# Gate logits of an attention + mixture-of-experts kernel, with gate weights and values swapped on TensorE

## The chip, the cores and the metric

One core of a Trainium2 chip runs the whole program. The metric is the device time of one execution in microseconds; smaller is better. TensorE is called PE below, its weight loads PEld, VectorE DVE, ScalarE ACT, GpSimd POOL, and SyncE, which here only issues transfers, SP.

## What is computed

The reference, cut to what matters:

```python
scores = scale * q @ k.T                     # 8 batches, 8 heads, 576 positions, head_dim 64
attn   = softmax(where(0 <= row - col < 64, scores, -1e9))
x      = (attn @ v) -> [4608, 512]           # heads side by side
logits = x @ w_gate                          # 8 experts
noisy  = logits + log1p(exp(x @ w_noise)) * noise
top2, top2_w = two largest of noisy, softmax over the two
out[row] += top2_w * (relu(x[row] @ w1[e]) @ w2[e])      # for the row's two experts
```

Everything is fp32. `x @ w_gate` and `x @ w_noise` together are 16 numbers for each row. Since `x` is a weighted sum of rows of `v`, the kernel multiplies `v` by the gate weights first (16 numbers for each key and head) and lets the attention weights sum those, as 16 extra columns beside the 64 value columns and one column of ones: attention's last product has 85 columns for a group of heads.

## The kernel before

The program has two stages. In the **attention stage** a loop over `j` (L761 on) handles 36 tiles: 9 blocks of 64 positions by 4 pairs of batches. One step of the loop holds parts of several tiles, so that each engine finds work: scores of tile `j`, softmax of `j` and `j-1`, transposes of `j-1`, the product with the values of `j-2`, normalising and the gate of `j-3`, storing `j-4`. Each engine executes its own instructions in the order in which the program issues them. In the **expert stage**, from about 182 us on, the eight experts' products run on PE, three chunks of rows for each expert, with rows gathered by POOL's indirect transfers.

In one step, PE's order is: `scores(j)` (L264, 16 matmuls on 64 x 64 quarters of the array), `pv(j-2)` (L323, 32 matmuls on such quarters), `transp(j-1)` (L300, four 128 x 128 transposes), `logits(j)` (L234). The trace shows two rows for each fp32 matmul, each with its weight load, and one for a transpose.

`logits(j)` is four matmuls. Stationary is one 128 x 128 slice of the turned values `VT` (128 contraction rows: two heads' dims, and 128 columns: the 64 keys of each of the pair's two sequence halves), moving are 64 gate-weight columns `wgx_sb`. The result is [128 keys, 256] in the shared PSUM tile `ps_g`, of which each half of the partitions needs half of the columns. `logits_copy(j)` (L240) takes the needed halves with two ACT copies of 64 partitions x 128 elements into slot 4 of the value tile `VW`, which `pv(j)` reads two steps later.

The softmax of a tile crosses the engines in this order: ACT copies the scores (`soft_a`, L274), DVE puts in the other block's columns (`soft_max`, L282) and takes the maximum (L287), POOL subtracts it (L288), ACT takes the exponential (`soft_b`, L292, in the step after), PE transposes (L300), DVE multiplies by the two masks (`apply_mask`, L305), PE takes the product with the values (L323, in the step after that). ACT's order in one step is `soft_b(j-1)`, `soft_a(j)`, eight scalings `norm_b(j-3)` (L342), the two copies L240, and, in steps 8 to 15, splitting an expert's weights (L215). Work of routing (L422 to L479) and POOL's scatters of row numbers (L482) are put between these in fixed portions.

SP issues the loads of queries (L93), keys (L97), values (L106), turned values (L112, for tile `j+2` into one of two buffers, after `logits(j)` has read it) and the stores of rows (L345).

Of the kernel before, what the change touches and what calls it, by code (L numbers as in the profile page):

```python
# [8 lines left out]
F32 = mybir.dt.float32  # L9
# [4 lines left out]
AF = mybir.ActivationFunctionType  # L14
# [49 lines left out]
def tile_kernel(ctx, tc, qT, kT, vx, vT, wgx, noise, w1, w2, out):  # L64
    nc = tc.nc
# [16 lines left out]
    wk = at.enter_context(tc.tile_pool(name="wk", bufs=2))  # L82
# [4 lines left out]
    VW = [acon.tile([128, 2, 5, 2, 4, 17], F32, name=f"vw{j}") for j in range(NP)]  # L87
    QC, VT = {}, {}

    def load_q(j):  # L90
        i, bp = divmod(j, NP)
        QC[j] = ld.tile([128, H, 64], F32, name="qc", bufs=3)
        nc.sync.dma_start(QC[j], qT[bp, :, i])  # L93

    def load_k(j):
        i, bp = divmod(j, NP)
        nc.sync.dma_start(KW[:, bp, i % 2], kT[bp, :, i])  # L97
# [6 lines left out]
    def load_v(j):  # L104
        i, bp = divmod(j, NP)
        nc.sync.dma_start(VW[bp][:, i % 2, 0:4], vx[bp, i])  # L106


    def load_vt(j):
        i, bp = divmod(j, NP)  # L110
        VT[j] = ld.tile([128, 4, 128], F32, name="vt", bufs=2)
        nc.sync.dma_start(VT[j], vT[bp, i])  # L112
# [3 lines left out]
    wgx_sb = acon.tile([128, 2, 64], F32)  # L116
# [11 lines left out]
    idle = ps.tile([128, 512], F32, name="ps_g")  # L128

    def warm(n):  # L130
        for _ in range(n):
            nc.tensor.matmul(idle[:, 384:512], lhsT=ones, rhs=ones, start=True, stop=True)

    warm(10)
    ident = consts.tile([128, 128], F32)
# [70 lines left out]
    def load_w1(e, ks=slice(0, KD), fs=slice(0, F)):  # L206
        if e < E:
            nc.sync.dma_start(w1s[:, ks, fs], w1[e][:, ks, fs])

    def load_w2(e, ks=slice(0, KF)):  # L210
        if e < E:
            nc.sync.dma_start(w2s[:, ks], w2[e][:, ks])
# [10 lines left out]
        return [lambda f=f: split(w2s[:, f], W2["h"][:, f], W2["l"][:, f]) for f in range(KF)]  # L223


    VG = idle[:, 0:256].rearrange("p (n c) -> p n c", n=1)

    def logits(j):
        p = VG[:, 0]
        x = VT.pop(j)  # L230
        for u in range(2):
            for g in range(2):
                q = u * 2 + g
                nc.tensor.matmul(p[:, q * 64:q * 64 + 64], lhsT=x[:, q, :], rhs=wgx_sb[:, g], start=True, stop=True)  # L234

    def logits_copy(j):
        i, bp = divmod(j, NP)
        for a in range(2):
            h = slice(a * 64, a * 64 + 64)
            nc.scalar.activation(VW[bp][h, i % 2, 4, :, :, 0:16].rearrange("p u (g x) e -> p (u g) x e", x=2),  # L240
                                 VG[h, 0].rearrange("p (k a x e) -> p k a x e", a=2, x=2, e=16)[:, :, a], AF.Copy)

    ST, T, P, TP, PT, XT = {}, {}, {}, {}, {}, {}

# [340 lines left out]
    def turn(e, c):  # L585
        pool = (exa, EXB.get("p"))[work.index((e, c)) % 2]
        xh = pool.tile([128, KD, WIDE], F32R, name="xh")
        xl = pool.tile([128, KD, WIDE], F32R, name="xl")
        XH[e, c], XL[e, c] = xh, xl
        cur = {}  # L590

        def f(q, m):
            if e:
                y = exa.tile([128, m // 32, KD, 32], F32, name="xy", bufs=2)
                nc.vector.transpose(y.rearrange("p t k c -> p (t k c)"),
                                    XG[e, c, q][:, :m // 32].rearrange("p t d -> p (t d)"))
                cur[q] = y.rearrange("p t k c -> p k t c")
            else:
                y = turn_bank()[:, :KD * m].rearrange("p (k m) -> p k m", k=KD)
                for k in range(KD):  # L600
                    nc.tensor.transpose(y[:, k], XG[e, c, q][:m, k * 128:k * 128 + 128], ident[:m, :m])
                cur[q] = y.rearrange("p k (t c) -> p k t c", c=32)

        def g(q, m):
            h, l = (x[:, :, q * 128:q * 128 + m].rearrange("p k (t c) -> p k t c", c=32) for x in (xh, xl))
            nc.scalar.activation(h, cur[q], AF.Copy)  # L606
            nc.vector.tensor_tensor(l, cur[q], h.bitcast(F32), op=OP.subtract)  # L607
        return [lambda q=q, m=m, x=x: x(q, m) for q, m in tiles(c) for x in (f, g)]
# [90 lines left out]
    def drain(n):  # L699
        calls[0] += 1  # L700
        while n and pending and calls[0] > calls[1]:
            f = next(pending[0], None)
            if f == HOLD:
                calls[1] = calls[0] + f
            elif f:
                f()
                n -= 1
            else:
                pending.pop(0)
# [5 lines left out]
    def drain_slots(n):  # L715
        for f in slots[:n]:
            f()
        del slots[:n]
# [4 lines left out]
    def ahead(n):  # L723
        for _ in range(n):
            if j >= NT and len(taken) < AHEAD:
                next(up00)
                taken.append(1)


    def rate(q):  # L730
        n = next(b for a, b in RATE if j < a)
        return (q + 1) * n // SLOTS - q * n // SLOTS
# [5 lines left out]
    def on(f, j, *a):  # L738
        if 0 <= j < NT:
            f(j, *a)  # L740

    for j in range(NT + 3):
        if j == TURN:
            for q, f in enumerate(turn(0, 0)):
                aux.setdefault(j + q // 2, []).append(f)

        if 0 < j < NT - 3:
            load_k(j + 3)
        on(store, j - 4)
        if j < 2:  # L750
            load_v(j + 2)
        if NT - 2 <= j < NT + 2:
            load_w2(0, slice((j - NT + 2) * 2, (j - NT + 3) * 2))
        on(norm_a, j - 3)
        drain(rate(0))
        on(scores, j)
        if j < NT - 3:
            load_q(j + 3)
        if W1G // 2 - 4 <= j < W1G // 2 + 4:
            k = j - W1G // 2 + 4  # L760
            load_w1(0, slice(k // 2, k // 2 + 1), slice(k % 2 * F // 2, (k % 2 + 1) * F // 2))  # L761
        if 2 < j < 3 + len(REST):
            REST[j - 3]()
        on(soft_b, j - 1)
        on(soft_a, j)
        ahead(2)
        drain(rate(1))
        on(pv, j - 2)
        on(norm_b, j - 3, 0)
        on(soft_max, j)  # L770
        on(soft_max2, j)
        drain_slots(1)
        if j < NP:
            warm(WARM)
        on(transp, j - 1)
        ahead(2)
        on(logits, j)
        if j < NT - 2:
            load_vt(j + 2)
        on(norm_b, j - 3, 1)  # L780
        on(apply_mask, j - 1)
        drain(rate(2))
        on(logits_copy, j)
        ahead(2)
        on(gate, j - 3)
        drain(rate(3))
        drain_slots(1 + j % 2)
        for f in aux.get(j, ()):
            f()
        drain(rate(4))  # L790
# [174 lines left out]
```

## Time and profile before

| | |
|---|---|
| Time, median of 3 runs | 1070.56 us (1070.03 to 1078.17) |
| Span of the profiled execution, first to last instruction | 1073.4 us |
| Attention stage, first to last `logits` of the 36 steps | 7.8 to 180.9 us |
| PE busy / PEld busy | 94% / 84% of the span |
| DVE / ACT / POOL busy | 41% / 38% / 50% of the span |
| Moved by DMA | 133.42 MB, 124 GB/s over the span |

How to read it: a row of a timeline gives the start in us, the duration, engine, line, operation, tile written <- tiles read, how many instructions were merged, and in brackets the idle time ahead of it with what ended that. A row of a group gives busy time, mean ns of one, and the idle time before. Windows give the busy time of each engine in a stretch, the granted PE clock (1.00 is full speed), and the mean busy share of the 16 DMA engines. Ends of matmuls are modelled, so starts are compared with starts.

### The profile page before, as it was taken

Reading aid. Unit: us, or ns where it says so; the run is one execution under the profiler, and the core shown is the slowest. Engines: PE = TensorE matmul, PEld = TensorE weight load, DVE = VectorE, ACT = ScalarE, POOL = GpSimd, SP = SyncE. Lnnn points to the kernel's source line nnn. Section 1 sums busy time; section 2 is a strip of 40 time slices with the busy share of each in tenths; the row PEclk is TensorE's granted clock in tenths of the full one; section 3 lists DMA queues with packets and bytes.
Section 4 is the critical chain, followed back from the end, with each engine's and each line's share of the span. In section 5 each row is a group of like instructions: output and inputs, shape, how many; then the busy total and the mean of one; then the engine's idle time right before and its main releaser. Section 6 shows DMA issues by size and latency. Waiting matters only on the chain. (4 is left out here: it accounts for less than half of the span.)

```text
span 1073.4 us, 19954 instructions
## 1 busy us (share of the span) xinstructions
PE 1012.5 (94%) x8025; PEld 906.9 (84%) x8025; DVE 444.7 (41%) x943; ACT 403.1 (38%) x1011; POOL 534.6 (50%) x612
## 2 busy tenths in 40 slices
PE   9877888899969999999999999999999999999993
PEld 8767877778859898889888988898889988998893
DVE  6687867621334325332633162326232523352220
ACT  5886766422333225222522252225222422342220
POOL 4445637574366543644365445453555454555411
PEclk9999989999989999999999999999999999999997
DMA  9998998499444234423452354235422541233212
GB/s 346 326 324 241 249 253 231 115 260 201 133 124 136 49 45 118 133 49 47 115 141 41 52 129 125 45 51 133 115 50 49 171 90 36 50 52 54 38 20 32
DMA packets 63255, 133.42 MB, mean 124 GB/s; under 512 B 16840, under 2 KB 17330, under 8 KB 61362
## 3 DMA queue, kind: packets, MB, share of 16 engines
q1 hardware_dynamic: 40562, 92.11, 27.2%
q0 software_dynamic: 22592, 39.95, 21.5%
q8 instruction: 65, 1.06, 0.4%
q14 instruction: 36, 0.29, 0.1%
HBM read 92.31 MB, written 39.70 MB: 123 GB/s over the span
## 5 line engine op out<-in xcount | busy, mean ns | idle before, releaser
L580 POOL DMA_INDIRECT xg<-xrows,ixs x266 | 257.4, 968 | 81.1 <-issue 76.0
L647 PE MATMUL ps_u<-xh,w1h 128*128 128x384 f32 (+1 forms) x752 | 260.7, 347 | 11.1 <-ACT xh L606 10.7
L662 POOL DMA_INDIRECT out_dram<-yo,lts x70 | 112.6, 1608 | 298.5 <-ACT yo L682 151.3
L648 PE MATMUL ps_u<-xl,w1h 128*128 128x384 f32 (+1 forms) x752 | 260.6, 347 | 0.0
L649 PE MATMUL ps_u<-xh,w1l 128*128 128x384 f32 (+1 forms) x752 | 260.2, 346 | 0.0
L677 PE MATMUL ps_d<-w2h,hh 128*128 128x512 f32 x576 | 224.7, 390 | 0.0
L679 PE MATMUL ps_d<-w2h,hl 128*128 128x512 f32 x576 | 224.5, 390 | 0.0
L678 PE MATMUL ps_d<-w2l,hh 128*128 128x512 f32 x576 | 224.4, 390 | 0.0
L654 DVE SCALAR_TENSOR_TENSOR hl<-ps_u,hh 128x384 fp32r<-128x384 f32 x188 | 104.6, 557 | 271.1 <-ACT hh L653 271.1
L653 ACT ACTIVATE hh<-ps_u 128x384 fp32r<-128x384 f32 x188 | 92.5, 492 | 239.6 <-PE ps_u L649 239.4
L647 PEld LDWEIGHTS ps_u<-xh,w1h 128*128 128x128 f32 x752 | 142.0, 189 | 16.9 <-ACT xh L606 11.6
L648 PEld LDWEIGHTS ps_u<-xl,w1h 128*128 128x128 f32 x752 | 141.9, 189 | 5.4 <-DVE xl L607 0.9
L649 PEld LDWEIGHTS ps_u<-xh,w1l 128*128 128x128 f32 x752 | 141.9, 189 | 3.7
L677 PEld LDWEIGHTS ps_d<-w2h,hh 128*128 128x128 f32 x576 | 108.1, 188 | 23.6 <-issue 1.8
L679 PEld LDWEIGHTS ps_d<-w2h,hl 128*128 128x128 f32 x576 | 108.1, 188 | 22.7
L678 PEld LDWEIGHTS ps_d<-w2l,hh 128*128 128x128 f32 x576 | 108.1, 188 | 21.8
L682 ACT ACTIVATE yo<-ps_d,lts 128x512 f32<-128x512 f32 x63 | 43.4, 690 | 196.0 <-PE ps_d L679 116.5
L607 DVE TENSOR_TENSOR xl<-xy,xh 128x512 fp32r<-128x512 f32 (+1 forms) x70 | 46.7, 667 | 148.2 <-ACT xh L606 148.2
L482 POOL DMA_INDIRECT slots<-val,posi x72 | 70.1, 974 | 17.8 <-issue 13.9
L288 POOL TENSOR_TENSOR t<-t,mx 128x512 f32<-128x512 f32 x36 | 37.6, 1043 | 73.5 <-DVE mx L287 67.0
L323 PE MATMUL ps_o<-vw,pt 64*64 64x85 f32 x2176 | 55.6, 251 | 14.7 <-issue 12.3
L342 ACT ACTIVATE x<-ps_o,r 128x80 f32<-128x80 f32 x288 | 67.0, 347 | 4.8 <-DVE r L334 4.2
(153 smaller groups left out, 968.4 us busy)
## 6 DMA issues: line engine op xcount, KB each, us to landing
w2s<-in_w_dram SPq DMA_DIRECT2D x7, 2048.0 KB
w1s<-in_w_dram SPq DMA_DIRECT2D x7, 2048.0 KB
vw<-in_vx_dram SPq DMA_DIRECT2D x36, 272.0 KB
out_dram<-zero SPq DMA_DIRECT2D x37, 256.0 KB
qc<-in_qT_dram SPq DMA_DIRECT2D x36, 256.0 KB
KW<-in_kT_dram SPq DMA_DIRECT2D x36, 256.0 KB
vt<-in_vT_dram SPq DMA_DIRECT2D x36, 256.0 KB
xrows<-x SPq DMA_DIRECT2D x36, 256.0 KB
```

What stands on the lines that cost most here:

```text
L342: nc.scalar.activation(XT[j][:, :, a * 4 + k], o[:, k, :, 0:16], AF.Copy, scale=r[:, k:k + 1])
L482: s = nc.gpsimd.indirect_dma_start(out=L, out_offset=bass.IndirectOffsetOnAxis(ap=posi[:, c2, q:q + 1], axis=0), in_=val[:, c2, q, :], in_ ...
L580: nc.gpsimd.indirect_dma_start(out=XG[e, c, t // 4][:, t % 4, :], out_offset=None, in_=XQ[:(DUMP + seen.get((e, c), NT) * 128) * 4], in_of ...
L647: nc.tensor.matmul(p[:, :n], lhsT=w1h[:, k, fs], rhs=xh[:, k, :n], start=(k == 0), stop=False)
L648: nc.tensor.matmul(p[:, :n], lhsT=w1h[:, k, fs], rhs=xl[:, k, :n], start=False, stop=False)
L649: nc.tensor.matmul(p[:, :n], lhsT=w1l[:, k, fs], rhs=xh[:, k, :n], start=False, stop=(k == KD - 1))
L653: nc.scalar.activation(h, p[:, :main], AF.Relu)
L654: nc.vector.scalar_tensor_tensor(l, p[:, :main], 0.0, h.bitcast(F32), op0=OP.max, op1=OP.subtract)
L662: nc.gpsimd.indirect_dma_start(out=out[:DUMP + seen.get((e, c), NT) * 128], out_offset=bass.IndirectOffsetOnAxis(ap=LT[e, c][:m, q, 0:1], ...
L677: nc.tensor.matmul(p, lhsT=hh[f][:, sl], rhs=w2h[:, f, :], start=(f == 0), stop=False)
L678: nc.tensor.matmul(p, lhsT=hh[f][:, sl], rhs=w2l[:, f, :], start=False, stop=False)
L679: nc.tensor.matmul(p, lhsT=hl[f][:, sl], rhs=w2h[:, f, :], start=False, stop=(f == KF - 1))
```

## The change

`logits(j)` swaps the operands: the gate weights are stationary, 32 columns at a time, and the turned values move, 64 keys at a time. Four such matmuls (`q` = 0 to 3) write the four groups of 32 partitions of a [128, 128] result, for each of two key halves `a`: eight matmuls where there were four, and the result holds only what is needed, but turned (gate columns on partitions, keys along the row). One ACT copy of 128 x 128 brings it to SBUF (`ls`, two buffers). In the next step PE transposes it (`logits_turn(j-1)`, after `transp(j-1)` and ahead of `logits(j)`), and a second ACT copy of 128 x 128 (`logits_store(j-1)`, behind `logits_copy(j)`) puts it into slot 4 of `VW`. `pv` of that tile reads it in the step after. The three PSUM regions lie in the bank that `ps_g` already held.

```diff
-    VG = idle[:, 0:256].rearrange("p (n c) -> p n c", n=1)
+    LT_, LROW, LS = idle[:, 0:128], idle[:, 128:256], {}
     def logits(j):
-        p = VG[:, 0]
         x = VT.pop(j)
-        for u in range(2):
-            for g in range(2):
-                q = u * 2 + g
-                nc.tensor.matmul(p[:, q * 64:q * 64 + 64], lhsT=x[:, q, :], rhs=wgx_sb[:, g], start=True, stop=True)
+        for a in range(2):
+            ks = slice(a * 64, a * 64 + 64)
+            for q in range(4):
+                nc.tensor.matmul(LT_[q * 32:q * 32 + 32, ks], lhsT=wgx_sb[:, q % 2, a * 32:a * 32 + 32],
+                                 rhs=x[:, q, ks], start=True, stop=True)
     def logits_copy(j):
+        LS[j] = wk.tile([128, 128], F32, name="ls")
+        nc.scalar.activation(LS[j], LT_, AF.Copy)
+
+    def logits_turn(j):
+        nc.tensor.transpose(LROW, LS.pop(j), ident)
+
+    def logits_store(j):
         i, bp = divmod(j, NP)
-        for a in range(2):
-            h = slice(a * 64, a * 64 + 64)
-            nc.scalar.activation(VW[bp][h, i % 2, 4, :, :, 0:16].rearrange("p u (g x) e -> p (u g) x e", x=2),
-                                 VG[h, 0].rearrange("p (k a x e) -> p k a x e", a=2, x=2, e=16)[:, :, a], AF.Copy)
+        nc.scalar.activation(VW[bp][:, i % 2, 4, :, :, 0:16], LROW.rearrange("p (u k e) -> p u k e", u=2, e=16), AF.Copy)
...
         on(transp, j - 1)
         ahead(2)
+        on(logits_turn, j - 1)
         on(logits, j)
...
         on(logits_copy, j)
+        on(logits_store, j - 1)
```

## The prediction

> **What bounds the kernel now.** I read the page first, then the windows over the stretches of the attention stage, then one undisturbed step in order of time, then the waits.
>
> ```profile
> PE 1012.5 (94%) x8025; PEld 906.9 (84%) x8025; DVE 444.7 (41%) x943; ACT 403.1 (38%) x1011; POOL 534.6 (50%) x612
> ...
> PEclk9999989999989999999999999999999999999997
> DMA  9998998499444234423452354235422541233212
> ...
> q8 instruction: 65, 1.06, 0.4%
> ```
>
> ```profile
> L234 PE MATMUL ps_g<-wgx_sb,vt x288: 222/275/421, 7.8 to 180.9; 128*128 128x64 f32 x144
> ```
>
> ```profile
> 8.00:26.00 18.00, 17.54 (x381) 16.20 (x379) 10.81 (x22) 11.38 (x38) 6.61 (x8) 1.00 1.04 389
> 26.00:60.00 34.00, 29.36 (x754) 25.93 (x753) 24.44 (x54) 28.31 (x101) 15.77 (x19) 0.95 0.98 339
> 60.00:90.00 30.00, 24.43 (x645) 22.21 (x645) 23.54 (x62) 22.75 (x83) 10.39 (x14) 0.94 0.84 269
> 90.00:134.00 44.00, 35.55 (x919) 32.04 (x922) 34.92 (x94) 30.77 (x112) 30.89 (x50) 0.96 0.97 256
> 134.00:161.00 27.00, 23.11 (x517) 20.76 (x510) 18.24 (x53) 17.97 (x64) 10.44 (x17) 0.81 0.97 253
> 161.00:182.00 21.00, 17.12 (x446) 15.28 (x446) 18.40 (x51) 15.79 (x54) 15.57 (x24) 1.00 0.90 264
> 182.00:1073.00 891.00, 858.51 (x4327) 767.95 (x4325) 309.66 (x599) 274.91 (x565) 439.36 (x451) 0.99 0.40 91
> ```
>
> PE's 94% over the span is an average of two different stages. After 182 us PE is busy 858.51 of 891 us: that part is PE's, and the change does not touch it. All that the change edits lies ahead of it: `logits` runs 36 times (288 rows, eight to a step) between 7.8 and 180.9 us, so a step takes 173.1 / 35 = 4.95 us on the average. There the DMA engines, at shares of 0.84 to 1.04, are as full as PE, and DVE is at 0.88 of the last stretch. So the first question is not how many microseconds PE saves, but how often PE is the last one in this stage. One undisturbed step shows its work:
>
> ```profile
> 87.72 1.10 PE L264 MATMUL ps_s<-KW,qc 64*64 64x128 f32 x32
> 88.65 1.36 PE L323 MATMUL ps_o<-vw,pt 64*64 64x85 f32 x64
> 89.94 0.66 PE L300 MATMUL ps_t<-ident,p 128*128 128x128 f32 x4
> 90.43 1.00 PE L234 MATMUL ps_g<-wgx_sb,vt 128*128 128x64 f32 x8
> 91.36 1.10 PE L264 MATMUL ps_s<-KW,qc 64*64 64x128 f32 x32
> 92.89 1.41 PE L323 MATMUL ps_o<-vw,pt 64*64 64x85 f32 x64 [0.42 <-issue]
> ```
>
> Start to start, scores take 0.93 us, the product with the values 1.29, the transposes 0.49, `logits` 0.93: 3.64 us of PE work in a step of 4.95. So 1.31 us of the average step is not PE's work at full clock. Even in this step PE waits at 92.89: the masks of that tile were still being written.
>
> ```profile
> 91.58 1.22 DVE L305 TENSOR_TENSOR pt<-ps_t,maskT 128x1024 f32<-128x1024 f32 x1
> ```
>
> They end at 92.80, 0.09 us ahead of the product. What drives DVE there is a ring that PE is no part of, by the groups between 8 and 182 us:
>
> ```profile
> L342 ACT ACTIVATE x<-ps_o,r 128x80 f32<-128x80 f32 x264 | 61.2, 348 | 2.9 <-DVE r L334 2.2 <-issue 0.3 <-DVE r L333 0.2
> ...
> L288 POOL TENSOR_TENSOR t<-t,mx 128x512 f32<-128x512 f32 x36 | 37.6, 1043 | 73.5 <-DVE mx L287 67.0 <-DMA xrows<-x 4.1 <-ACT vw L240 1.5
> ...
> L287 DVE TENSOR_REDUCE mx<-t 128x8 f32<-128x512 f32 x36 | 24.7, 686 | 1.2
> ...
> L282 DVE COPY_PREDICATED t<-mprev,ps_s 128x512 f32<-128x512 uint32 x32 | 23.3, 730 | 18.4 <-ACT t L274 11.6 <-POOL w1l L216 6.2 <-issue 0.2
> L292 ACT ACTIVATE p<-t 128x512 f32<-128x512 f32 x35 | 21.8, 623 | 9.9 <-POOL spacer L481 7.1 <-POOL t L288 2.5
> L240 ACT ACTIVATE vw<-ps_g 64x128 f32<-64x128 f32 x72 | 19.7, 274 | 33.1 <-PE ps_g L234 32.3
> L274 ACT ACTIVATE t<-ps_s 128x512 f32<-128x512 f32 x32 | 19.1, 597 | 2.2 <-PE ps_s L264 1.5
> ```
>
> Maximum of tile `j` (0.686), subtraction on POOL (1.043), exponential on ACT (0.623), behind which ACT's order puts the score copy of tile `j+1` (0.597), then DVE's two passes over that (0.730, and the maximum again): 3.68 us a step before any hand-off, where PE needs 3.64. The two are level. Work taken from PE alone cannot bring an undisturbed step much below what it is.
>
> Where PE is late, the waits tell:
>
> ```profile
> ACT vw L240 <- PE ps_g L234: 32.3, 18, 6.9
> PEld ps_o L323 <- issue: 14.0, 13, 3.7
> DVE t L282 <- ACT t L274: 11.6, 13, 1.6
> ...
> ACT p L292 <- POOL spacer L481: 7.1, 7, 1.3
> ...
> PEld ps_g L234 <- DMA vt<-in_vT_dram: 4.9, 5, 1.6
> ```
>
> In 18 of 36 steps ACT stood waiting for `logits` to end; in the other half it came to the copy later than PE. The 18 are the steps in which a shorter `logits` can be felt. But many of them are late for reasons that a shorter `logits` does not remove: the load of `vt` (five waits), and pauses in the middle of the 64 rows of L323, where nothing in the profile is waited for:
>
> ```profile
> 80.62 0.51 PE L323 MATMUL ps_o<-vw,pt 64*64 64x85 f32 x11 [2.98 <-issue]
> ```
>
> ```profile
> 106.48 1.98 PE L323 MATMUL ps_o<-vw,pt 64*64 64x85 f32 x47 [3.58 <-issue]
> ```
>
> ```profile
> 141.01 2.14 PE L323 MATMUL ps_o<-vw,pt 64*64 64x85 f32 x50 [2.10 <-issue]
> ```
>
> During the second of these, in the transfers from 102.7 to 106.4 us, stands one packet of instructions, while the data queue keeps the engines full:
>
> ```profile
> q1 hardware_dynamic: 726, 1.34, 102.8%
> q0 software_dynamic: 96, 0.00, 2.1%
> q8 instruction: 1, 0.02, 1.6%
> ```
>
> I read the pauses as PE waiting for its next instructions; the trace shows the coincidence, not the cause. They sum to 8.7 us, and the stretches that hold them lose granted clock besides: 0.06 x 30 = 1.8 us, 0.04 x 44 = 1.8, 0.19 x 27 = 5.1.
>
> **The change, part by part** (per step, on PE from start to start).
>
> Removed: `logits` as it is, 0.93 us.
>
> Added, the turn: one transpose, a quarter of 0.49 = 0.12.
>
> Added, the eight matmuls on 32 columns: 16 load-and-multiply pairs, in four rounds of four groups. No row shows groups of 32 columns. The nearest are the quarters: 32 rows with 128 moving columns take 0.93, so 0.116 for four at once; 64 rows with 85 columns take 1.29, 0.081 for four. The slope is 0.035 / 43 columns, which gives 0.064 for four rows with 64 columns, and 4 x 0.064 = 0.26 us. That is the lower end. The upper end is that nothing overlaps: 16 pairs at today's 0.93 / 8 = 0.116 make 1.86. The quarters share their array rows two by two and differ in their columns, which is the arrangement of the change, and four of them still cost 0.081; so I take the value near the lower end, 0.30.
>
> Added, a change of the array's shape: today the shape changes between `logits` and `scores` and between the product and the transposes; the change puts one more between turn and `logits`. Its price shows here:
>
> ```profile
> 90.94 0.50 PE L234 MATMUL ps_g<-wgx_sb,vt 128*128 128x64 f32 x3
> ```
>
> Three rows in 0.50 us, the last of 0.275 (the median above): a pitch of 0.112, and the last starts at 91.165. The scores follow at 91.36, 0.195 later, 0.08 over the pitch. Bounds 0 and 0.25, taken 0.15, since a first load is not hidden.
>
> Sum: -0.93 + 0.12 + 0.30 + 0.15 = **-0.36 us a step**, x 36 = -13.0 us if PE were last in every step. With the low prices (0.26, 0.08) it is -0.47, -17 us; with no overlap at all (1.86) +1.20, +43 us.
>
> In a sentence by itself: the Trainium skill, page "TensorE: Matmul & The Clock Gate", Part 3, "The mechanism", says that a weight load overlaps running matmuls only where its group of array rows is another one, and all four 32-column groups span the same 128 rows; by it the loads would stand between the matmuls, as a result of its own, which is a rival below. This trace speaks against it as far as it goes, since in L323 quarters that share their rows are loaded 64 times in 1.29 us.
>
> ACT: two copies of 128 elements a partition before (L240, 274 ns), two copies of 128 elements after; on twice the partitions, at an unchanged length. I cost it at zero; the bounds are -0.05 and +0.10 us a copy around the 0.274, since a shorter row of 80 elements on all 128 partitions, the scaling L342, takes 0.348. What is new is a wait: `pv` now needs the store that ACT does in the step just before, behind the copy that waits for `logits`. Behind this `pv` on PE wait its transposes, `logits` and the next scores. The chain is copy 0.27 + store 0.27 + some 0.1 for each of two hand-offs = 0.75 us, and its cover is the next scores, 0.93 us on PE, and the masks, which end later in the step shown. If ACT comes late, as in half of the steps, its two copies end when they ended before, because their sum is the same. So nothing is added where the masks are last; without that cover, at most 0.27 in a step.
>
> Transfers: none is added or moved. SP issues `vt` for tile `j+2` when `logits(j)` is done, as before, now up to 0.36 us earlier. It goes into DMA engines that are already 0.95 busy, so I give it nothing.
>
> Instructions: 8 + 8 rows and loads become 16 + 16, and the turn adds 2: 18 a step, 648 in all. The queue's 1.06 MB for 2 x 8025 rows is 66 bytes for each, so 43 KB, or 2.6 packets of the size 1.06 MB / 65 = 16 KB. The stage needs some 30 today (3662 of the 8025 rows) and pauses 8.7 us in three of them; at 0.3 us for each packet that is +0.8 us.
>
> **What of it passes on.** The 18 steps of 36 in which ACT waited for `logits` are the upper share, one half. In the 26 to 60 us stretch and before it (some 13 steps) the data rate stands at 339 to 389 GB/s and the DMA share at 0.98 to 1.04: there an earlier PE only waits for its loads. Scaling the half by the 23 steps that are left, 18 x 23 / 36 = 11.5 steps, x 0.36 = 4.1 us. With the packets: -4.1 + 0.8 = -3.3 us. The end of the stage moves the expert stage with it one to one, since PE is 0.96 busy there.
>
> The profiled span is 1073.4 us, 2.8 over the median of the runs, inside their spread; the forecast for the span is 1070.1, and the same difference from the median gives **1067.3 us**. A measurement of this kernel tells about 1% (10.7 us) from no change, so I expect no change that can be told.
>
> **The rivals.**
>
> 1. *All of it passes on.* PE is last everywhere, and the saving is 13 to 17 us: 1054 to 1058. For it: in 18 steps ACT waits for PE, and pauses leave PE behind for steps on end. Against it: the ring of 3.68 us, the product's wait for the masks, the DMA share.
>
> 2. *The four column groups do not overlap* (the side of slower). Place: the sixteen pairs of `logits`. It decides once they take more than 0.93 - 0.12 - 0.15 = 0.66 us a step. If loads shrink with their columns (an estimate: half of a pair's 0.116 is load, a quarter of that is left, 0.073) the pairs take 1.16, and a step's PE work is 3.64 + 0.50 = 4.14, above the ring; passing on 0.6 of 36 x 0.50 = 18 us gives +11: 1081. With nothing shrunk, +43 x 0.8: 1105. The skill's rule of the row groups is this rival. For it: no row shows 32-column groups. Against it: the quarters.
>
> 3. *Nothing passes on.* Loads and the ring hide all of it, and only the packets are left: +0.8, 1071.4.
>
> 4. *More pauses.* Each of the 2.6 further packets falls on a full queue, costs 3 us and 1.7 us of granted clock, as most of today's did: 2.6 x 4.7 = +12.2, less the 4.1 of the forecast: 1078.7. For it: three such pauses in 30 packets. Against it: the other 27.
>
> **How the numbers follow.** Forecast 0.48, rival 1 0.14, rival 2 0.10, rival 3 0.20, rival 4 0.08. Faster by over 1% (below 1059.9): rival 1 and 0.02 of the forecast's tail, 0.16. Slower by over 1% (above 1081.3): most of rival 2 and a third of rival 4, 0.12. Within: 0.72. The range leaves out the fast part of rival 1 and most of rival 2: 1057 to 1080.
>
> **What would show each step right or wrong.** The transposes of the turn at 0.12 and the eight matmuls at about 0.30 from start to start, with 16 rows in rounds of four; a gap of 0.1 to 0.2 ahead of them; ACT's two copies still at some 0.27; the product waiting for the masks in more steps, and longer, than now; fewer than 18 waits of ACT for `logits`; the DMA share of the stage above 0.95 by as much as the stage is shorter; about 68 packets of instructions. The prediction is wrong if sixteen pairs take over 0.66 us, if `pv` waits for the store on ACT, or if the stage's last `logits` comes before 170 or after 190 us where it was 180.9.

## The result, and the profile after

The changed kernel takes 1077.92 us (median of 20 runs, 1071.64 to 1080.98), the kernel before, run beside it, 1073.99 (20 runs, 1069.43 to 1081.73): a ratio of 1.0052, 95% interval 1.0035 to 1.0068. It is slower by half a per cent, where a gain of 0.3% was forecast. Ratios, here and below, are worked out from the executions in the faster of two states that the chip shows, medians from all of them, so that the two need not divide exactly. The profiled execution has a span of 1075.1 us, against 1073.4.

The page of the changed kernel, to be held against the first fence of the prediction:

```profile
PE 1002.3 (93%) x8349; PEld 888.8 (83%) x8349; DVE 444.3 (41%) x943; ACT 396.2 (37%) x1011; POOL 534.5 (50%) x612
...
q8 instruction: 68, 1.11, 0.4%
```

PE is busy for 10.2 us less and has 324 more rows and as many more loads, and the instruction queue has 68 packets in place of 65: all as expected. Now one step in order of time, with the lines of the new kernel (L327 is the product, L304 the transposes, L241 the turn, L233 the gate matmuls, L268 the scores):

```profile
89.10 0.66 PE L304 MATMUL ps_t<-ident,p 128*128 128x128 f32 x4
89.59 0.27 PE L241 MATMUL ps_g<-ident,ls 128*128 128x128 f32 x1
89.79 0.43 PE L233 MATMUL ps_g<-vt,wgx_sb 128*32 128x64 f32 x16
90.16 1.10 PE L268 MATMUL ps_s<-KW,qc 64*64 64x128 f32 x32
91.12 2.35 PE L327 MATMUL ps_o<-vw,pt 64*64 64x85 f32 x64
```

From the turn's start to the scores' start 0.57 us pass, where 0.93 passed before: the step is shorter by 0.36 us, exactly the forecast, and most steps of the trace agree to 0.01 us. Yet the stage ends later. The rows of `logits`, which were at 180.9 us for the last one, and the stage as one stretch, first the kernel before, then the changed one:

```profile
L233 PE MATMUL ps_g<-vt,wgx_sb x576: 216/219/316, 8.0 to 187.4; 128*32 128x64 f32 x192
```

```profile
8.00:182.00 174.00, 147.12 (x3641) 132.41 (x3640) 130.33 (x331) 126.95 (x445) 89.67 (x130) 0.94 0.95 289
```

```profile
8.00:182.00 174.00, 134.71 (x3923) 112.74 (x3927) 126.52 (x326) 118.01 (x435) 88.24 (x127) 0.93 0.94 287
```

PE was busy for 12.4 us less in the same 174 us, and in that time DVE and ACT got through less work, not more (326 instructions for 331, 435 for 445). So PE's saved time has become idle time of PE, and more. The granted clock is no reason: 0.93 for 0.94 over the stretch. The loss builds up late. Up to the 21st tile the transposes of the changed kernel start now earlier than before (2.7 us for the 17th tile), now later (1.2 us for the 15th). From the 22nd on they start later each time, and 2.7 us later for the 35th. The rest of the 6.5 us at the last `logits` is one pause of PE inside them, the longest of all:

```profile
187.07 0.64 PE L233 MATMUL ps_g<-vt,wgx_sb 128*32 128x64 f32 x12 [3.66 <-issue]
```

The waits between 8 and 182 us tell where it went:

```profile
ACT ls L238 <- PE ps_g L233: 38.9, 21, 6.4
PEld ps_o L327 <- issue: 20.6, 23, 2.8
PE ps_o L327 <- issue: 15.9, 15, 2.7
PEld ps_g L233 <- DMA vt<-in_vT_dram: 8.2, 5, 3.8
PEld ps_g L233 <- issue: 8.0, 29, 2.4
...
PEld ps_o L327 <- ACT vw L245: 1.0, 1, 1.0
```

ACT waits for PE in 21 steps (18 before). The new wait for the store on ACT is there once, for 1.0 us; before, PE waited 2.1 us there, in three steps. The five waits for the turned values take 8.2 us, where five took 4.9. What grew most is "issue": PE's loads for the product stand still for 20.6 us in 23 places (14.0 in 13), and its loads for `logits` for another 8.0 (1.4 before), with nothing waited for that the profile shows. These are the pauses of the prediction. Six of them, in the timeline of PE:

```profile
63.42 1.25 PE L327 MATMUL ps_o<-vw,pt 64*64 64x85 f32 x54 [0.87 <-issue]
...
68.27 1.10 PE L327 MATMUL ps_o<-vw,pt 64*64 64x85 f32 x44 [0.89 <-issue]
...
73.55 0.95 PE L327 MATMUL ps_o<-vw,pt 64*64 64x85 f32 x35 [1.43 <-issue]
...
83.04 0.60 PE L327 MATMUL ps_o<-vw,pt 64*64 64x85 f32 x18 [1.06 <-issue]
...
88.79 0.38 PE L327 MATMUL ps_o<-vw,pt 64*64 64x85 f32 x8 [1.94 <-issue]
...
96.78 0.55 PE L304 MATMUL ps_t<-ident,p 128*128 128x128 f32 x3 [3.06 <-issue]
```

They come further forward in the step each time: 54, 44, 35, 18, 8 rows of the product are left. That is what a limit in the count of instructions looks like when a step has a little less than the limit. The windows from one pause to the next count them (PE's rows and PE's loads are the first two numbers in brackets):

```profile
63.30:68.10 4.80, 3.95 (x127) 3.26 (x126) 4.66 (x12) 3.91 (x14) 2.52 (x4) 1.00 0.89 295
68.10:73.40 5.30, 3.85 (x126) 3.26 (x127) 4.43 (x12) 4.38 (x18) 1.04 (x1) 1.00 0.92 290
73.40:82.90 9.50, 7.62 (x253) 6.49 (x253) 6.83 (x21) 6.23 (x26) 2.08 (x2) 1.00 0.89 290
82.90:88.60 5.70, 3.81 (x127) 3.20 (x126) 5.46 (x15) 5.10 (x21) 3.57 (x7) 1.00 0.90 262
```

127 + 126 = 253 each time, and three semaphore events of PE that this view does not count: 256. The third window holds two such blocks, of which the first ended without a pause. One packet of instructions is 1.11 MB / 68 = 16 KB, or 64 bytes for each of 256. Up to 185 us, counting PE's rows, loads and semaphore events in order of start, every pause of PE of over 0.3 us for which neither PE nor its loads have a releaser (but two before, of 0.7 us together) stands at the same place of a block of 256, in the kernel before as in the changed one. Before, 11 of 29 such limits have a pause of over 0.25 us, 13.8 us in all from start to start; after, 19 of 31, 29.7 us. Counted narrowly, as time in which PE neither loads nor multiplies, it is 12 us before and 24 after. The pause of 3.66 us in the last `logits` stands at a limit too, but beyond the 185 us, and comes on top. What PE waits for lies in the transfers between 94.3 and 96.8 us, ahead of the last pause above:

```profile
q1 hardware_dynamic: 526, 0.96, 101.8%
q8 instruction: 1, 0.02, 2.4%
```

One packet of instructions, among data that fill the engines. In the records it begins at 94.42 us, and PE goes on at 96.78, 2.36 us later; at the other five pauses the distance is 2.2 to 2.4 us as well (61.17 to 63.42, 66.04 to 68.26, 71.22 to 73.55, 80.69 to 83.04, 86.55 to 88.79). From 15 us on, at every other limit of the two traces with an idle time of over 0.15 us, the one in the last `logits` among them, the distance is 2.2 to 2.6 us too; and where PE goes over a limit without a pause, its packet began at least 2.2 us before. So a pause there ends with the arrival of the packet. The packet for a block begins only after PE has gone over the limit ahead of it, on the average 4.0 us to the packet's end. So a block that PE crosses faster than its successor arrives ends in a pause. Not counting the pauses, PE took 5.42 us for a block on the average before and 4.67 after.

The expert stage gives some of it back. Its first product starts at 189.4 us against 183.0, 6.4 later; after 520 rows of products PE is 2.7 us behind (318.3 against 315.6). Ahead of that row lies one long wait for ACT's part of the next rows, by the waits from 265 to 320 us, before and after:

```profile
PE ps_u L647 <- ACT xh L606: 9.7, 1, 9.7
```

```profile
PE ps_u L651 <- ACT xh L610: 7.4, 1, 7.4
```

So the end of the attention stage does not move the expert stage one to one, as the prediction had it; that is why 6.5 us at the last `logits` are 1.7 us of the span, in a single execution, and 3.9 us between the medians.

### The profile page after: what moved, and what is told of

The parts are those of the page before. It is cut to its first block, busy times and chain, and to the rows that moved or that the text cites. A ratio compares the mean times of both kernels' runs of the same rounds, so it can differ in the third digit from the quotient of the medians.

```text
span 1075.1 us, 20600 instructions
## 1 busy us (share of the span) xinstructions
PE 1002.3 (93%) x8349; PEld 888.8 (83%) x8349; DVE 444.3 (41%) x943; ACT 396.2 (37%) x1011; POOL 534.5 (50%) x612
## 3 DMA queue, kind: packets, MB, share of 16 engines
q8 instruction: 68, 1.11, 0.4%
## 5 line engine op out<-in xcount | busy, mean ns | idle before, releaser
L651 PEld LDWEIGHTS ps_u<-xh,w1h 128*128 128x128 f32 x752 | 141.9, 189 | 14.5 <-ACT xh L610 9.3
L327 PE MATMUL ps_o<-vw,pt 64*64 64x85 f32 x2176 | 56.7, 247 | 19.0 <-issue 15.9
L327 PEld LDWEIGHTS ps_o<-vw,pt 64*64 64x64 f32 x2176 | 49.9, 142 | 24.9 <-issue 20.9
```

The lines of the kernel that those rows point to most:

```text
L327: nc.tensor.matmul(PO[j][u * 64:u * 64 + 64, a, g * 2 + x, :], lhsT=pt[pa, w, u * 2 + g, x * 64:x * 64 + 64], rhs=v[pa, (i + w) % 2, :, u, ...
L651: nc.tensor.matmul(p[:, :n], lhsT=w1h[:, k, fs], rhs=xh[:, k, :n], start=(k == 0), stop=False)
```

## The experiments

Two theories stand in the expectations. **F**, the limit: PE cannot cross blocks of 256 instructions faster than they arrive beside full data transfers; the change makes PE faster and gives it 18 more instructions a step (234 for 216), so it meets the limit more often, and the saved time is waited off there. **W**, work and waits: the turn, the new order of the arrays, the later store or PE's own time hold the stage. "Pauses" below are those at the block limits up to 185 us, counted as above.

All experiments but the last two ran where the kernel before itself takes 1154 to 1197 us, and not 1074, so each is to be read against the kernel before beside it. (In the trace b_again of that condition the granted clock is 0.85 from 8 to 182 us, where it was 0.94.) Pauses and last `logits` come from one profiled execution of each; that of a_again took 1183.93 us, 8 us over its median.

**The change once more, with half of the matmuls, and the old kernel with more instructions.** The second computes only half of the gate columns (each twice) with four matmuls of 128 moving columns, so that turn, copies and order stay, with 218 instructions a step; the third adds five one-column matmuls to the kernel before (236 a step), into unused columns; the fourth adds one 128 x 128 matmul a step to the changed kernel.

```diff
-        for a in range(2):
-            ks = slice(a * 64, a * 64 + 64)
-            for q in range(4):
-                nc.tensor.matmul(LT_[q * 32:q * 32 + 32, ks], lhsT=wgx_sb[:, q % 2, a * 32:a * 32 + 32],
-                                 rhs=x[:, q, ks], start=True, stop=True)
+        for q in range(4):
+            nc.tensor.matmul(LT_[q * 32:q * 32 + 32], lhsT=wgx_sb[:, q % 2, 0:32], rhs=x[:, q], start=True, stop=True)
```

```diff
         pt, v = PT.pop(j), VW[bp]
+        for t in range(5):
+            r, c = slice(t % 2 * 64, t % 2 * 64 + 64), slice(t // 2 % 2 * 64, t // 2 % 2 * 64 + 64)
+            nc.tensor.matmul(o[c, t % 2, 400:401], lhsT=ones[r, 0:64], rhs=ones[r, 0:1], start=True, stop=True)
```

```diff
-        if j < NP:
-            warm(WARM)
+        if j < NT:
+            warm(WARM if j < NP else 1)
```

The changed kernel (a_again):

> The changed kernel once more, beside the others. Theory F (instructions): PE executes blocks of 256 instructions (16 KB); a block can run only some 5.4 us after the block before it began, while the transfers are full, and the change puts 234 instructions into a step where 216 were. Expected again: ratio 1.003 to 1.008, pauses of PE at the block limits of 28 to 38 us in the attention stage (13.8 before). Theory W (a new wait or the shape of the array): the same ratio, but the pauses vary freely.

Half of the matmuls (a_half):

> The change with four matmuls of 128 moving columns in place of eight of 64: the first half of the gate weights is used for both key halves, so half of the gate logits are other numbers. Turn, two copies, late store, four 32-column groups and the PE time stay; 18 instructions a step instead of 34 (16 before). F: pauses fall back to 10 to 20 us, the saved PE time is seen: ratio 0.988 to 0.998 of before. W: nothing that it names is taken away, so 1.003 to 1.008 as the change itself.

More instructions in the kernel before (b_tiny):

> The kernel before with five further matmuls of one column on 64 x 64 quarters at the head of the values' product, into unused columns: 20 more instructions a step, some 0.1 us of PE work, no wait, no change of shape. F: pauses rise to 25 us or more, ratio 1.005 to 1.013. W: at most the PE work, 36 x 0.1 = 3.6 us and of that a third: 1.000 to 1.002.

More work in the changed kernel (a_warm):

> The changed kernel with one unused 128 x 128 matmul ahead of the turn in steps 4 to 35: 4 more instructions and some 0.33 us of PE work a step, 10.6 us in all. F: PE's work fills its pauses, which shrink by 4 to 8 us, and the time grows by 0 to 5 us over the changed kernel. W (PE's work decides): 6 to 11 us more.

| | us (before beside it) | ratio, 95% | pauses, us | last `logits`, us |
|---|---|---|---|---|
| a_again | 1175.93 (1184.95) | 0.9951, 0.9908 to 0.9993 | 22.8 | 203.6 |
| a_half | 1172.69 (1184.95) | 0.9919, 0.9879 to 0.9958 | 12.4 | 200.4 |
| b_tiny | 1181.02 (1184.95) | 0.9991, 0.9945 to 1.0037 | 6.1 | 207.4 |
| a_warm | 1182.54 (1184.95) | 1.0010, 0.9962 to 1.0058 | 7.8 | 204.8 |

Here the change is a gain of 0.5%, the opposite sign. The half of the matmuls is a little better still, with the same turn, store and order, which speaks for F; but the two intervals overlap. The instructions added to the kernel before cost nothing that can be told, against a simple price for each instruction. Most numbers of F missed here: it had 1.005 and more and pauses of 25 us for b_tiny, and 0 to 5 us over the changed kernel for a_warm, which took some 7 us more, as W had it. Both theories had counted on the 1074 us of the result.

**Lighter transfers.** Queries are loaded for the first tile alone and keys for the first two blocks, and these are used again in all steps, so that a step loads and stores 512 of its some 1300 KB less; all products keep their size.

```diff
+        if j == 0:
+            QC["one"] = acon.tile([128, H, 64], F32, name="qc")
+            nc.sync.dma_start(QC["one"], qT[0, :, 0])
+        QC[j] = QC["one"]
...
-        nc.sync.dma_start(KW[:, bp, i % 2], kT[bp, :, i])
+        if i < 2:
+            nc.sync.dma_start(KW[:, bp, i % 2], kT[bp, :, i])
```

The kernel before with it (b_light):

> The kernel before with one tile of queries for all steps and the keys of the first two blocks only: 512 of 1296 KB of loads and stores fewer in a step, with other attention weights as a result. F (instructions come late because transfers are full): pauses of PE at the block limits fall from 13.8 to under 6 us, the stage ends 10 to 40 us sooner, ratio 0.965 to 0.99. W: sooner too, but it says nothing on pauses.

The changed kernel with it (a_light):

> The changed kernel with the same lighter loads. F: its pauses fall from 33 to under 12 us, and it is now faster than the lighter kernel before by 3 to 13 us, since the saved PE time is no longer eaten. W: its wait or its shape is still there, so it stays slower than the lighter kernel before by 3 to 8 us.

The kernel before with one more 128 x 128 matmul a step (b_warm):

> The kernel before with one unused 128 x 128 matmul ahead of the gate logits in steps 4 to 35: 4 more instructions and some 0.33 us of PE work a step, 10.6 us in all: more PE work than five small matmuls, a fifth of their instructions. F: +1 to +5 us, less than the five small ones. W (PE's work decides): more than the five small ones.

b_light took 1156.84 us beside 1163.08 (0.9966, 0.9921 to 1.0011), with pauses of 0.9 us; a_light 1144.47 (0.9835, 0.9762 to 0.9907), pauses 10.1, last `logits` at 186.5 against 195.9; b_warm 1166.85 (1.0038, 0.9997 to 1.0078). With lighter transfers the change is worth 12.4 us between the medians, with the same turn and the same later store. That does not show that the full transfers take the gain away: in this condition the change was a gain with full transfers as well (a_again, 0.9951), and 0.9835 / 0.9966 = 0.9869 cannot be told from that, given the intervals. What the traces show is an earlier arrival: the DMA share from 8 to 182 us is 0.67 in a_light for 0.89 in a_again, and a packet ends 3.0 us on the average after PE has gone over the limit ahead, for 4.0. The pauses are 9.2 us more than in b_light here too, and the stage ends 9.4 us earlier all the same. The work added in b_warm costs some 4 us, within F's 1 to 5, but more than the five small matmuls, as W had it.

**Three of them once more, on another chip.**

Half of the matmuls (n_half):

> The four-matmul form of the change (half of the gate weights used twice, so half of the gate logits are other numbers; 18 instructions a step instead of 34) again, where the kernel before takes about 1074 us. F: pauses of PE at the block limits 10 to 20 us, ratio 0.988 to 0.998. W: 1.003 to 1.008 as the change itself.

More instructions in the kernel before (n_tiny):

> The kernel before with five one-column matmuls (20 more instructions a step, some 0.1 us of PE work) again, where it takes about 1074 us. F: pauses 25 us or more, ratio 1.005 to 1.013. W: 1.000 to 1.002.

More work in the changed kernel (n_warm):

> The changed kernel with one unused 128 x 128 matmul a step (4 more instructions, some 0.33 us of PE work) again, where the kernel before takes about 1074 us. F: 0 to 5 us over the changed kernel, ratio 1.005 to 1.010, pauses 4 to 8 us shorter than its 33. W (PE's work decides): 6 to 11 us over the changed kernel, ratio 1.011 to 1.016.

1166.81 us (0.9870, 0.9822 to 0.9918), 1182.72 (1.0015, 0.9980 to 1.0049) and 1180.88 (0.9979, 0.9945 to 1.0013) beside 1183.91: the same picture. The 1074 us that their expectations name did not come; n_tiny lies at W's number, and n_warm is below both.

**The kernel before, traced in the same condition.**

The kernel before against itself (b_again):

> The kernel before itself, for its trace beside those of the experiments, where it takes 1163 to 1185 us. F: its pauses at block limits are under those of the changed kernel there (22.8 us), at 5 to 15 us, and its stage is the longer one by 0 to 10 us. W: no statement on pauses; the stage is as long or shorter than the changed kernel's.

One look at more instructions (p_tiny2):

> The kernel before with five one-column matmuls (20 more instructions a step), one look. F, where the kernel before takes about 1074 us: pauses at the block limits of 20 us or more and a stage 5 to 12 us longer than 180.9; where it takes about 1180 us, pauses of 5 to 8 us as seen twice. W: no more pauses than the kernel before has.

b_again took 1183.69 us beside 1185.29 (0.9990, 0.9926 to 1.0054). Its pauses at block limits are 4.2 us, but between 88 and 190 us PE stands still 35 times elsewhere in its blocks, 22.1 us in all, against twice and 0.7 us in the first trace of this kernel. They look like this, with POOL's scatters of row numbers beside them:

```profile
103.30 0.98 POOL L482 DMA_INDIRECT slots<-val,posi  x1 [0.16 <-issue]
...
104.58 0.96 POOL L482 DMA_INDIRECT slots<-val,posi  x1 [0.21 <-issue]
...
104.62 0.30 PE L323 MATMUL ps_o<-vw,pt 64*64 64x85 f32 x2 [0.39 <-issue]
...
105.37 0.36 PE L323 MATMUL ps_o<-vw,pt 64*64 64x85 f32 x3 [0.44 <-issue]
...
106.11 0.40 PE L323 MATMUL ps_o<-vw,pt 64*64 64x85 f32 x4 [0.38 <-issue]
```

So PE is slower between the limits (6.60 us for a block), comes to them late, and in most cases the next block is there. That this is why the change gains in this condition is a reading of the traces; no run shows it by itself. p_tiny2, a single run, took 1185.74 us beside 1170.46 for one run of the kernel before, with pauses of 3.6 us, where F had 5 to 8.

**Without the scatters.** To be rid of these short pauses, the 72 scatters are left out, so that the lists of rows keep their padding and the expert stage adds to no row.

```diff
-        slots.extend(lambda c2=c2, q=q: scatter(c2, q) for q in range(n) for c2 in range(2))
+        slots.extend(lambda: None for q in range(n) for c2 in range(2))
```

The kernel before (s_before):

> The kernel before without the 72 scatters of row numbers: the lists keep their padding, so every expert works on padding rows, with the same instructions otherwise. It takes away POOL's transfers and the short pauses of PE beside them. F: from tile 17 on a step costs 216 / 256 of a block at some 5.2 us, 4.4 to 4.7 us, pauses at the block limits 10 to 25 us in the stage. W: a step is set by loads, PE and the softmax ring, 3.7 to 4.2 us, with few pauses.

The changed kernel (s_after):

> The changed kernel without the scatters. F: 234 / 256 of a block, 4.7 to 5.0 us a step from tile 17 on, its stage ends 2 to 8 us later than that of the kernel before without scatters, pauses 12 to 25 us longer. W (without another wait): it ends 2 to 8 us sooner, since PE has 0.36 us less in a step.

Half of the matmuls (s_half):

> The four-matmul form of the change (half of the gate weights used twice) without the scatters: 218 instructions a step, PE time as in the change. F: its stage ends with that of the kernel before without scatters, 3 us about it, and 2 to 8 us ahead of the change's. W: as the change's, within 2 us.

More instructions in the kernel before (s_tiny):

> The kernel before with five one-column matmuls a step and without the scatters: 236 instructions a step. F: its stage ends 4 to 12 us later than without the five. W: 0 to 2 us later.

| | us | ratio, 95% | pauses, us (limits with one) | last `logits`, us |
|---|---|---|---|---|
| s_before | 1082.38 | 0.9326, 0.9275 to 0.9377 | 8.3 (9 of 30) | 176.1 |
| s_after | 1087.29 | 0.9351, 0.9296 to 0.9407 | 24.6 (23 of 32) | 175.3 |
| s_half | 1079.40 | 0.9313, 0.9257 to 0.9369 | 14.5 (12 of 31) | 167.0 |
| s_tiny | 1083.96 | 0.9358, 0.9299 to 0.9416 | 13.8 (16 of 33) | 175.5 |

Without the scatters all four take 75 to 83 us less than the kernel before beside them, but every expert then works on padding rows, so this is no price of the scatters.

At the end of the stage the case of the result is back: the change saves 13 us of PE's work, and the stage ends only 0.8 us earlier, with 16.3 us more of pauses. The totals say little on it. The trace of s_after is of its longest execution, 1093.91 us; it is 0.9 us behind that of s_before at the 1000th row of products, and 12.7 at the last, in a part that the change does not touch. The rows that carry the comparison, changed and half:

```profile
L233 PE MATMUL ps_g<-vt,wgx_sb x576: 216/219/313, 7.8 to 175.3; 128*32 128x64 f32 x192
```

```profile
L231 PE MATMUL ps_g<-vt,wgx_sb x288: 269/297/422, 7.5 to 167.0; 128*32 128x128 f32 x144
```

Half of the instructions of `logits`, longer each (a median of 297 ns for 219), but the group takes 0.36 us from start to start in both, and the stage ends 8.3 us earlier. W has no place for that. F missed two things: it had the change end later than s_before, and in s_tiny 20 more instructions a step brought 5.5 us more of pauses, as it said, but no later end. It may be that where PE has not been made faster, a pause at a limit is taken out of waits that it would have had anyway; no run shows that. The four totals' intervals overlap; what is concluded rests on the ends of the stage, one trace each.

**A version with fewer instructions that computes everything.** Four matmuls with 128 moving columns (both sequence halves at once) in place of eight; the turned result then has its halves in other places, and four ACT copies of 64 x 64 put them right where one of 128 x 128 did: 218 instructions of PE a step, more work on ACT.

```diff
-            ks = slice(a * 64, a * 64 + 64)
-            for q in range(4):
-                nc.tensor.matmul(LT_[q * 32:q * 32 + 32, ks], lhsT=wgx_sb[:, q % 2, a * 32:a * 32 + 32],
-                                 rhs=x[:, q, ks], start=True, stop=True)
+            for g in range(2):
+                c = a * 64 + g * 32
+                nc.tensor.matmul(LT_[c:c + 32], lhsT=wgx_sb[:, g, a * 32:a * 32 + 32],
+                                 rhs=x[:, g::2, a * 64:a * 64 + 64], start=True, stop=True)
...
-        nc.scalar.activation(VW[bp][:, i % 2, 4, :, :, 0:16], LROW.rearrange("p (u k e) -> p u k e", u=2, e=16), AF.Copy)
+        for u in range(2):
+            for a in range(2):
+                h = slice(a * 64, a * 64 + 64)
+                nc.scalar.activation(VW[bp][h, i % 2, 4, u, :, 0:16],
+                                     LROW[u * 64:u * 64 + 64, h].rearrange("p (k e) -> p k e", e=16), AF.Copy)
```

The whole kernel (c_swap):

> The whole computation with four matmuls of 128 moving columns for each tile in place of eight of 64, so 218 instructions of PE a step as in the run with half of the gate weights, and four ACT copies of 64 x 64 behind the turn in place of one of 128 x 128 (some 0.6 us a step more on ACT, which waits for PE in most steps). Limit theory: the pauses at the block limits fall to 11 to 15 us and the last logits come at 199 to 203 us where the kernel before takes some 1184 us; ratio to before 0.990 to 0.994, some 3 us below the changed kernel's 0.995. Rival, work on ACT decides the stage: three more copies of some 0.22 us are 24 us over the 36 steps, of which the half in which ACT is behind passes on; ratio 1.000 to 1.006.

The same without the scatters (s_swap):

> The same without the 72 scatters (the lists of rows keep their padding), to be compared with the three runs without scatters: before 181 us for the last logits, changed 181, half 173. Limit theory: pauses 13 to 16 us, last logits at 173 to 176, total 1079 to 1083 us, below the 1082.4 of before and the 1087.3 of the change. Rival, work on ACT decides: last logits at 181 to 190, total 1085 to 1095.

c_swap ran where the kernel before takes 1071.49 us (13 runs), the condition of the result, and took 1068.15 (10 runs, 1064.9 to 1070.77): 0.9960, 0.9936 to 0.9984. It is faster than the kernel before by 0.4%, and, by way of that kernel, 0.9% faster than the changed kernel, which was at 1.0052 (1.0035 to 1.0068). Its pauses are 11.0 us at 7 of 30 limits. One step, its last `logits` and its waits:

```profile
80.90 0.27 PE L241 MATMUL ps_g<-ident,ls 128*128 128x128 f32 x1
81.10 0.43 PE L233 MATMUL ps_g<-vt,wgx_sb 128*32 128x128 f32 x8
81.46 1.10 PE L272 MATMUL ps_s<-KW,qc 64*64 64x128 f32 x32
```

```profile
L233 PE MATMUL ps_g<-vt,wgx_sb x288: 269/273/297, 7.5 to 175.7; 128*32 128x128 f32 x144
```

```profile
ACT ls L238 <- PE ps_g L233: 16.7, 10, 5.9
...
PEld ps_o L331 <- ACT vw L248: 13.7, 17, 1.0
...
PEld ps_o L331 <- issue: 6.0, 5, 2.3
```

PE's part of the step is 0.56 us, as in the changed kernel, and the product now waits for the store on ACT in 17 steps, 13.7 us, a loss that W counts. Still the stage ends 11.7 us earlier than in the changed kernel (175.7 against 187.4; 7.6 us at the transposes of the 35th tile), with 18.7 us less of pauses. Part of these are gone because PE, held by ACT, comes to the limits later (5.56 us for a block), not because there are fewer of them. The ratio lies above F's 0.990 to 0.994 and below the 1.000 to 1.006 of the rival of this run, that ACT decides; with its interval the rival falls. s_swap took 1050.55 us beside 1071.49 (0.9788, 0.9745 to 0.9831), with pauses of 9.5 us and the last `logits` at 169.3; it ran where the kernel before takes 1071 us and not 1162, so neither theory's numbers can be held against it. (The 181, 181 and 173 us in its expectation are the starts of the 36th tile's transposes; the last `logits` came at 176.1, 175.3 and 167.0.)

## Why the prediction was wrong

- **The local sum** was right: -0.36 us a step, forecast and measured. The turn with the change of shape takes 0.20 (priced at 0.12 + 0.15), the sixteen pairs 0.37 (priced at 0.30): two errors of 0.07 us that cancel, so that the exact sum is luck. Sixteen pairs on four groups of 32 columns do overlap; rival 2 is out.
- **ACT's copies at nothing** held: 291 and 289 ns a copy against 274, and a wait for the store of 1.0 us in the whole stage.
- **"At 0.3 us for each packet that is +0.8 us"** is the step that failed. It priced a pause for each packet, as if pauses fell on packets by chance, and so let only the 2.6 new packets pay. But each block has a time of arrival: at every limit of the stage the question is who comes first, PE or the packet. PE's saving and its 18 further instructions a step brought it there first at 19 limits in place of 11, and the pauses up to 185 us rose by 15.9 us, not by 0.8 (by 12 us in the narrow count), and by 3.7 more with the one in the last `logits`. That is as much as the 13.0 us saved, or more. The prediction had the evidence ahead of it: it saw the coincidence of pause and packet, but added up three long pauses (8.7 us) and did not ask at which count of instructions they stood; 11 limits with 13.8 us were to be had from the same trace.
- **"x 0.36 = 4.1 us" of gain passes on** was not so: a lead of 3.1 us at the 21st tile was gone at the 22nd and did not come back. The ring of 3.68 us and the masks were not what stopped it, either: with the same ring a step takes 4.8 us on the average in c_swap and 4.6 in s_half, and 4.95 in the kernel before.
- **Rival 4** had the right mechanism and, at 1078.7 us, nearly the measured 1077.92, but by a wrong count: it made the new packets pay 4.7 us each, where eight more of the old limits paid 2 us each. That the count agrees is luck.
- **Rival 1 and rival 3** are out: the one by the sign, the other because a good deal more than 0.8 us was lost.

Of the tests that the prediction named, "fewer than 18 waits of ACT for `logits`" turned out the other way (21), and it is the one that showed at once that PE had become later, not earlier. Its three signs of being wrong did not come: the sixteen pairs stayed under 0.66 us, the wait for the store came once, for 1.0 us (2.1 before), and the last `logits` came at 187.4 us, inside 170 to 190.

What stays open: how large a part the full data transfers have, since no run delays the instructions alone; what makes the short pauses beside the scatters where the kernel before takes over 1150 us; and how the saved 13 us, the 18 instructions and the changed place of the limits in a step share the 15.9 us of pauses.

## What to carry to other kernels

Where data transfers are full, count PE's instructions as well as its time: a stage of small matmuls cannot run faster than its blocks of instructions arrive, and an edit that saves time by more and smaller matmuls pays there, once PE is the engine that is ahead. Look for pauses "issue" of PE in the middle of a group and count the instructions between two of them; if it is always the same number, take instructions out rather than time. A gain that was worked out per step needs the check that ACT or DVE wait for PE less often afterwards.

## What the runs showed of the hardware

- A packet of 16 KB holds 256 instructions of PE, weight loads, matmuls and semaphore events alike. Where PE waited at a limit, it went on 2.2 to 2.6 us after the packet's record began. The record began only after PE had entered the block ahead, and on the average a packet ended 3.0 us (lighter transfers, a_light) to 4.0 us (the changed kernel) after that moment.
- The Trainium skill, page "Runtime: NRT & Kernel Launch", section "Instruction fetch mechanics", says that engines get their instructions in blocks of 16 KiB, 256 of them, and that crossing a boundary is mostly hidden. The trace agrees on the block; here it was hidden at 12 of the 31 limits up to 185 us, and the other 19 cost 29.7 us of a stage of 179 us.
- Sixteen pairs of loads and matmuls on four groups of 32 columns, all on the same 128 rows, took 0.37 us, 23 ns a pair, where the eight pairs on the full array took 0.93, 116 ns a pair. With 128 moving columns the eight pairs of c_swap took 0.36 us, 45 ns each.
